# New durations in a planner's table, block sums of x on one engine, and a scaling step on either of two

## The chip, the cores and the metric

One NeuronCore of one Trainium2 chip runs the kernel. The metric is device time in microseconds (us) of one execution; lower is better. The engines are PE (TensorE), DVE (VectorE), ACT (ScalarE), POOL (GpSimd) and SP (the queue that issues most transfers). Each runs its own instructions strictly in the order in which the program wrote them.

## The reference

```python
def reference(q, k, v, n_sink, window, moe_*, moe2_*):
    x = attention(q, k, v)        # 2 batches, 8 heads, 768 rows, head size 64; window of 128 plus 4 sink columns
    x = x.reshape(1536, 512)
    # first mixture: every expert sees every row
    P = exp(x @ w_gate - max); P = 8 rounds of row and column scaling of P     # 1536 x 8
    x = sum(P[:, e:e+1] * (relu(x @ w1[e]) @ w2[e]) for e in range(8))         # 512 -> 1024 -> 512
    # second mixture: each row goes to one expert, 192 rows each, by a greedy pass over the sorted logits
    logits = x @ w_gate2
    out[rows of e] = relu(x[rows of e] @ w1b[e]) @ w2b[e]
```

All inputs and the output are float32.

## The kernel before

Rows of x are held in 12 tiles of 128 (the code's `t`), two tiles to a group of 256 columns, two groups to a pair `p` of 512. Every matmul operand is kept as a rounded high part and a low remainder (`hh`/`hl`, `w1hs`/`w1ls`, `xp[:, 0]`/`xp[:, 1]`), and each product is three matmuls: high by high, low by high, high by low. ACT makes high parts, DVE makes low parts by a subtraction.

The program runs through these stages. **Opening and attention**, over 12 tiles, with expert 0 of the first mixture woven in once two tiles of x are ready (`make_step`: first products G1 at L1037, second products G2 at L1068; `relu` and `hlo` make `hh` and `hl` at L1106 and L1109). Expert 0's output waits for the factors P: `cb` (L1082, ACT) copies it out of the accumulator, and `scale0` (L1089, DVE) multiplies it by P later. **Experts 1 to 5**, in 60 units (`make_unit`): the first product of a unit is seven block products of 2x2 blocks (L1272), which need sums and differences of blocks of x. `make_tx` makes these sums once for each of the three pairs p, eight 128x512 tensors for each (`to`: L1209 sums of a high and a low part, L1212 differences), and splits them into high and low (L1215 ACT, L1216 DVE). `split_blocks` does the same with the weights (L929 to L980). After a unit's products, ACT copies (`cp`, `cu`, L1288), DVE adds (`c`, L1296), ACT applies relu (L1329), DVE makes the low part (`hl`, L1332), and the second products follow (L1360). A unit's first product writes the buffer that the unit before has to have emptied, so PE waits there for the `hl<-hp` of L1332. **Experts 6 and 7**, in pairs (L1130), while DVE forms the second gate's logits (L1446, L1466). Then the **routing** rounds on DVE, with second products of expert 7 held back as cover for PE (L1068), rows scattered to memory by row number and read back, and the **second mixture**, 8 experts of 192 rows (L2025 to L2078). There an expert's two output halves are scattered by POOL (`out_dram`, L2102), with row numbers that DVE casts into `idx` (L1932); `idx` has three buffers, so the casts of an expert wait until the scatter of the expert three before has landed. Weights come in through SP, are split by ACT (L869) and DVE or POOL (L867) all along.

No order is written out by hand. Everything is a `task(engine, cost, function, deps, prio)`, and a planner (`Sched.run`), while the program is built, picks the next task by these costs; the order of the picks is the program order of each engine. A task may name two engines with two costs; the one on which it would end first gets it. The costs serve the planner alone: no instruction depends on them but through the order, the choice of engine, and this method, which puts transposes of the identity matrix (the fillers, L200) on PE where the planner expects PE to have nothing to do until time t:

```python
def warm(self, t):
    c = self.clock["PE"]
    free = [j for j in range(len(self.banks)) if self.banks[j] is not None and self.banks[j] <= c]
    per = 0.213 if c < COLD else 0.11
    n = int((t - c - 0.06) / per)
    if n < 1 or not (self.extra or free):
        return
    p = ps.tile([P, 512], F32, name=self.extra or self.names[free[0]])
    for _ in range(n):
        nc.tensor.transpose(p[:, :P], ident, ident)
```

A result reaches another engine `LAG` = 0.15 us after its cost has run (0.23 behind PE, 1.1 behind a transfer), in both kernels.

## Time and profile before

| what | us |
|---|---|
| median of 3 runs | 1386.44 |
| lowest and highest run | 1386.37, 1393.91 |
| the profiled execution, its own time | 1385.85 |
| its span, first to last instruction | 1383.9 |

All rows shown below come from the profiled execution; what lies around its span is 1385.85 - 1383.9 = 1.95 us. Its time is 0.6 us below the median. A row of the trace names the line of the code, the engine, the operation, output<-inputs, and partitions x elements; times in the timeline count from the start of the span.

### The profile page before, as it was taken

What the parts mean: (1) busy time and instruction counts of PE and PEld (TensorE: products, weight loads), DVE (VectorE), ACT (ScalarE), POOL (GpSimd) and SP (SyncE); (2) the same over time, 40 slices, a digit from 0 to 9 for tenths busy, and PEclk for the clock granted to TensorE, in tenths of its full rate; (3) what the DMA queues carried; (4) which work ended last, traced back from release to release, by engine and by line L of the source; (5) the groups of instructions that cost most, each with busy time, mean ns of one, the idle gap of its engine ahead of it and who ended that gap; (6) DMA issues with size and microseconds to landing.
All of it is one profiled execution on the core that took longest, in us unless ns stands there. A gap on an engine that the chain in (4) does not pass through costs nothing. (4 is left out here: it accounts for less than half of the span.)

```text
span 1383.9 us, 22562 instructions
## 1 busy us (share of the span) xinstructions
PE 1357.6 (98%) x8220; PEld 1166.5 (84%) x8220; DVE 940.0 (68%) x2538; ACT 622.8 (45%) x1570; POOL 124.2 (9%) x255
## 2 busy tenths in 40 slices
PE   8999999989999999999999999999999999999998
PEld 7888888879988888998888899888887777788876
DVE  8877765996364655546464645449999768578875
ACT  6877762544243433333342423331133353267764
POOL 3211110230000000000000000000001113410111
PEclk9999999999999999999999999999999999999999
DMA  7432311111020101011010101161020010478762
GB/s 177 123 83 57 85 39 39 62 49 59 16 62 1 62 16 47 16 46 47 16 49 14 62 1 61 46 200 41 16 92 16 1 46 17 118 248 273 244 218 70
DMA packets 102532, 101.50 MB, mean 73 GB/s; under 512 B 42248, under 2 KB 79112, under 8 KB 102288
## 3 DMA queue, kind: packets, MB, share of 16 engines
q1 hardware_dynamic: 100432, 93.71, 22.5%
q0 software_dynamic: 1984, 6.30, 1.4%
q8 instruction: 67, 1.10, 0.3%
q14 instruction: 49, 0.40, 0.1%
HBM read 91.71 MB, written 8.28 MB: 72 GB/s over the span
## 5 line engine op out<-in xcount | busy, mean ns | idle before, releaser
L1329 ACT ACTIVATE hh<-c 128x256 fp32r<-128x256 f32 x180 | 73.4, 414 | 128.0 <-DVE c L1296 114.9
L1130 PE MATMUL hp<-xp,w1hs 128*128 128x512 f32 x384 | 121.0, 396 | 0.0
L1296 DVE TENSOR_TENSOR c<-hp,cp 128x256 f32<-128x256 f32 x120 | 50.6, 422 | 101.2 <-PE hp L1272 100.3
L1360 PE MATMUL o<-w2ls,hh 128*128 128x512 f32 x240 | 95.1, 396 | 0.0
L1360 PE MATMUL o<-w2hs,hh 128*128 128x512 f32 x240 | 94.4, 393 | 0.0
L1360 PE MATMUL o<-w2hs,hl 128*128 128x512 f32 x240 | 94.3, 393 | 0.0
L1272 PE MATMUL hp<-xp,w1hs 128*128 128x256 f32 x480 | 89.1, 284 | 4.8 <-DVE hl L1332 4.5
L1272 PEld LDWEIGHTS hp<-xp,w1hs 128*128 128x128 f32 x480 | 78.1, 190 | 11.2 <-DVE hl L1332 5.6
L1535 POOL TENSOR_TENSOR hl<-h,hh 128x256 fp32r<-128x256 f32 x15 | 12.2, 815 | 803.4 <-ACT hh L1532 763.1
L1332 DVE SCALAR_TENSOR_TENSOR hl<-c,hh 128x256 fp32r<-128x256 f32 x180 | 76.6, 435 | 8.1 <-ACT hh L1329 5.3
L1130 PEld LDWEIGHTS hp<-xp,w1hs 128*128 128x128 f32 x384 | 69.4, 188 | 14.8
L1130 PE MATMUL hp<-xp,w1ls 128*128 128x512 f32 x192 | 75.9, 395 | 0.0
L1037 PE MATMUL hp<-xp,w1hs 128*128 128x256 f32 x384 | 74.0, 287 | 0.1
L1068 PE MATMUL o<-w2hs,hh 128*128 128x512 f32 x176 | 71.4, 406 | 0.0
L1068 PE MATMUL o<-w2hs,hl 128*128 128x512 f32 x176 | 69.9, 397 | 0.7 <-DVE hl L1109 0.6
L1068 PE MATMUL o<-w2ls,hh 128*128 128x512 f32 x176 | 70.0, 398 | 0.0
L1329 ACT ACTIVATE hh<-hp 128x256 fp32r<-128x256 f32 x60 | 23.1, 385 | 103.5 <-PE hp L1272 103.5
L867 DVE TENSOR_TENSOR w1ls<-w1r,w1hs 128x512 fp32r<-128x512 f32 x90 | 61.1, 688 | 11.8 <-ACT w1hs L869 11.1
L867 DVE TENSOR_TENSOR w2ls<-w2r,w2hs 128x512 fp32r<-128x512 f32 x89 | 59.2, 685 | 14.4 <-ACT w2hs L869 9.0
L1288 ACT ACTIVATE cu<-hp 128x256 f32<-128x256 f32 x60 | 22.9, 382 | 102.0 <-PE hp L1272 102.0
L1272 PE MATMUL hp<-xp,w1ls 128*128 128x256 f32 x240 | 68.1, 284 | 0.0
L1332 DVE SCALAR_TENSOR_TENSOR hl<-hp,hh 128x256 fp32r<-128x256 f32 x60 | 25.5, 424 | 59.9 <-ACT hh L1329 59.8
(490 smaller groups left out, 4067.0 us busy)
## 6 DMA issues: line engine op xcount, KB each, us to landing
w1r<-in_moe_w_dram SPq DMA_DIRECT2D x46, 512.0 KB, 4.3
w2r<-in_moe_w_dram SPq DMA_DIRECT2D x46, 512.0 KB, 4.4
wr<-in_moe_w_dram SPq DMA_DIRECT2D x46, 512.0 KB, 4.1
xs<-xs_d SPq DMA_DIRECT2D x14, 256.5 KB, 4.0
nk<-in_k_dram SPq DMA_DIRECT2D x12, 256.0 KB, 3.8
nq<-in_q_dram SPq DMA_DIRECT2D x12, 256.0 KB, 5.9
nv<-in_v_dram SPq DMA_DIRECT2D x12, 256.0 KB, 3.1
wgb<-wgd SPq DMA_DIRECT2D x1, 2048.0 KB
```

The source lines that it names most:

```text
L867: (nc.gpsimd if eng == "POOL" else nc.vector).tensor_tensor(lo[:, c], r[:, c], f32(hi[:, c]), op=OP.subtract)
L1037: nc.tensor.matmul(p, a, b, start=(c == 0 and j == 0), stop=(c == DC - 1 and j == 2), skip_group_check=True)
L1068: nc.tensor.matmul(OUTP[g, j], a_, b_, start=(first and i == 0), stop=(last and i == 2), skip_group_check=True)
L1130: nc.tensor.matmul(HS[k, 0].rearrange("p a b -> p (a b)"), a, b, start=(c == 0 and j == 0), stop=(c == DC - 1 and j == 2), skip_group_chec ...
L1272: nc.tensor.matmul(st[bk], l_[:, c], r_[:, c], start=(start and c == 0 and j == 0), stop=(c == 1 and j == 2), skip_group_check=True)
L1288: act(st[key], st[bk], AF.Copy)
L1296: tt(st[out], st[bk], st[key], op=OP.add)
L1329: act(hh, st[key], AF.Relu)
L1332: nc.vector.scalar_tensor_tensor(HT[i, f, t][1], st[key], 0.0, f32(HT[i, f, t][0]), op0=OP.max, op1=OP.subtract)
L1360: nc.tensor.matmul(OUTP[g, j % GT], a_, b_, start=(first and f == 0 and z == 0), stop=(last and f == 1 and z == 2), skip_group_check=True)
L1535: (nc.gpsimd if eng == "POOL" else nc.vector).tensor_tensor(HT[s][1], h32_of(g, fc), f32(HT[s][0]), op=OP.subtract)
```

## The change

Almost all costs in the planner's table are replaced. On DVE and ACT they rise: a 128x512 subtraction from 0.61 to 0.69, one of 128x256 from 0.34 to 0.43, ACT's 128x512 copies from 0.48 to 0.60 or from 0.52 to 0.63, the 128x256 ones from 0.27 or 0.31 to 0.39, the attention's small steps likewise. On PE those of the first expert, of the pairs and of the second mixture rise by some 6 to 9% (G2: 0.2157 to 0.2325 a matmul); the costs of the units' products (0.703 and 1.395), of POOL's subtractions (`PSP` 1.35) and of transfers stay. Two tasks change in kind: the block sums of x may no longer go to POOL, and the scaling of expert 0's output may go to ACT.

```diff
-        l0 = task("DVE", 0.61, lambda: low(0), deps=a + d, prio=pr, use=[KH[t]], name="klo")
+        l0 = task("DVE", 0.69, lambda: low(0), deps=a + d, prio=pr, use=[KH[t]], name="klo")
...
-            nms = [task(("DVE", "ACT"), (0.20, 0.30) if n == 1 else (0.27, 0.42), lambda eng, hp=hp, hh=hh: nm(eng, hp, hh), deps=[r], prio=pr, use=[eh, sth], name="norm")
+            nms = [task(("DVE", "ACT"), (0.28, 0.40) if n == 1 else (0.355, 0.51), lambda eng, hp=hp, hh=hh: nm(eng, hp, hh), deps=[r], prio=pr, use=[eh, sth], name="norm")
...
-                    l = task(("DVE", "POOL"), (0.61, PSP), lambda eng, k=k, c=c: sp(k, c, True, eng), deps=[a],
+                    l = task(("DVE", "POOL"), (0.69, PSP), lambda eng, k=k, c=c: sp(k, c, True, eng), deps=[a],
...
-                def scale0(j=j, t=t):
+                def scale0(eng, j=j, t=t):
                     a0 = acc[g][:, j, :DM]
-                    ts(a0, a0, PR[:, t, 0:1], None, op0=OP.mult)
+                    if eng == "ACT":
+                        act(a0, a0, AF.Copy, scale=PR[:, t, 0:1])
+                    else:
+                        ts(a0, a0, PR[:, t, 0:1], None, op0=OP.mult)
...
-                    CB[t] = task("DVE", 0.4, scale0, deps=[z, SKH[0]], prio=v_gem(NG * NU * 2 + s % 48), name="sc0")
+                    CB[t] = task(("DVE", "ACT"), (0.45, 0.62), scale0, deps=[z, SKH[0]], prio=v_gem(NG * NU * 2 + s % 48), name="sc0")
...
-            def go(eng):
+            def go():
...
-                f(nc.gpsimd if eng == "POOL" else nc.vector, s3(sm[nm]))
+                f(nc.vector, s3(sm[nm]))
 
-            x = task(("DVE", "POOL"), (0.61, PSP), go, deps=[SW["task"]] + [z[0] for z in deps], prio=pr + 0.1 * k,
+            x = task("DVE", 0.69, go, deps=[SW["task"]] + [z[0] for z in deps], prio=pr + 0.1 * k,
```

What follows for the order: fillers rise from 146 to 249. Of the 24 block sums, POOL had 11 and now has none. Of the 12 scalings DVE had all and now has 3. POOL takes 8 weight subtractions (L867) more from DVE, ACT 8 of DVE's normalizations of attention (L622), and DVE 11 copies of the transposed attention weights (L647) from ACT.

Vector engine, in units 1 and 2, from the add that ends a block product of unit 1 to the `hl<-hp` that unit 2's first product waits for; `sA`, `sB`, `wr`, `t` are block sums of x, `tx` and `xp` their low parts, `c` and `hl` belong to the unit. Before (the sums at L1209 and L1212 that don't stand here were POOL's):

```order
L1296 TENSOR_TENSOR c_3819<-hp_3735,cp_3798 128x256
L1212 TENSOR_TENSOR sB<-sA,wr 128x512
L1296 TENSOR_TENSOR c_3833<-side_3778,cu_3785 128x256
L1332 SCALAR_TENSOR_TENSOR hl<-c_3819,hh 128x256
L1216 TENSOR_TENSOR tx_3208<-wr,tx_3208 128x512
L1216 TENSOR_TENSOR tx_3208<-sB,tx_3208 128x512
L1216 TENSOR_TENSOR xp_122<-t_3837,xp_122 128x2x256
L1332 SCALAR_TENSOR_TENSOR hl<-hp_3735,hh 128x256
```

The same place in the changed kernel, vector engine again (lines from L1090 on stand three further down in it):

```order
L1299 TENSOR_TENSOR c_3895<-hp_3793,cp_3875 128x256
L1215 TENSOR_TENSOR wr<-wr,sA 128x512
L1299 TENSOR_TENSOR c_3908<-side_3858,cu_3865 128x256
L1335 SCALAR_TENSOR_TENSOR hl<-c_3895,hh 128x256
L1212 TENSOR_TENSOR sA<-xp_122 128x512
L1219 TENSOR_TENSOR tx_3219<-wr,tx_3219 128x512
L1335 SCALAR_TENSOR_TENSOR hl<-hp_3793,hh 128x256
```

Between the first add and the `hl<-hp` there were three low parts and one difference; there are one low part, one sum and one difference now, and the other sums stand ahead of or behind the piece.

TensorE, at the step from unit 1's first two block products to its third (`hp0<-tx0,ehs`); `av` is the second product of the unit before. Before:

```order
L1360 MATMUL av_3759<-w2hs2_143,hh_3711 128x512
L1360 MATMUL av_3759<-w2ls2_144,hh_3711 128x512
L1360 MATMUL av_3759<-w2hs2_143,hl_3712 128x512
L1360 MATMUL av_3759<-w2hs2_143,hh_3700 128x512
L1360 MATMUL av_3759<-w2ls2_144,hh_3700 128x512
L1360 MATMUL av_3759<-w2hs2_143,hl_3701 128x512
L1272 MATMUL hp0_3735<-tx0_3207,ehs1_3203 128x256 x2
```

The same step on TensorE in the changed kernel:

```order
L1363 MATMUL av_3815<-w2hs2_143,hh_3764 128x512
L1363 MATMUL av_3815<-w2ls2_144,hh_3764 128x512
L1363 MATMUL av_3815<-w2hs2_143,hl_3765 128x512
L1363 MATMUL av_3815<-w2hs2_143,hh_3748 128x512
L1363 MATMUL av_3815<-w2ls2_144,hh_3748 128x512
L1363 MATMUL av_3815<-w2hs2_143,hl_3749 128x512
L200 MATMUL side0_3834<-ident_82 128x128 x16
L1275 MATMUL hp0_3793<-tx0_3218,ehs1_3214 128x256 x2
```

Sixteen fillers stand ahead of the third block product where there were none. In all, units 0 to 3 had 17 fillers and have 62; the later units had none and have eight times 2; ahead of the first G1 there were 114 and are 152.

Vector engine, second mixture, from the output of the fifth expert (`yb`) to the casts of the row numbers of the eighth (`idx`), which wait for that output's scatter. Before:

```order
L2098 TENSOR_TENSOR yb<-side_15901,yb 64x512
L867 TENSOR_TENSOR w2ls_136<-w2r,w2hs_135 128x512
L867 TENSOR_TENSOR w1ls_138<-w1r,w1hs_137 128x512
L867 TENSOR_TENSOR w2ls_136<-w2r,w2hs_135 128x512
L867 TENSOR_TENSOR w2ls_140<-w2r,w2hs_139 128x512
L2042 TENSOR_TENSOR sm<-av,t_16170 128x192
L867 TENSOR_TENSOR w2ls_140<-w2r,w2hs_139 128x512
L2051 SCALAR_TENSOR_TENSOR hs<-sm,hs 128x128
L2052 SCALAR_TENSOR_TENSOR hs<-sm,hs 128x64
L2042 TENSOR_TENSOR sm<-side_16161,t_16181 128x192
L1932 CAST idx_16207<-xs_15772 128x1
L1932 CAST idx_16209<-xs_15774 64x1
```

Vector engine in the changed kernel, the twelve rows that end with the same casts (the fifth expert's `yb` stands nine rows ahead of the first of them):

```order
L867 TENSOR_TENSOR w1ls_138<-w1r,w1hs_137 128x512
L2054 SCALAR_TENSOR_TENSOR hs<-sm,hs 128x128
L2055 SCALAR_TENSOR_TENSOR hs<-sm,hs 128x64
L867 TENSOR_TENSOR w1ls_138<-w1r,w1hs_137 128x512
L2045 TENSOR_TENSOR sm<-side_16282,t_16334 128x192
L867 TENSOR_TENSOR w2ls_140<-w2r,w2hs_139 128x512
L2054 SCALAR_TENSOR_TENSOR hs<-sm,hs 128x128
L2055 SCALAR_TENSOR_TENSOR hs<-sm,hs 128x64
L867 TENSOR_TENSOR w2ls_140<-w2r,w2hs_139 128x512
L2045 TENSOR_TENSOR sm<-hp_16321,t_16359 128x192
L1935 CAST idx_16374<-xs_15902 128x1
L1935 CAST idx_16376<-xs_15904 64x1
```

The second cast moved from 11 to 20 rows behind the `yb` whose scatter it waits for; between them stand seven subtractions of `hs` and `sm` steps more and one weight subtraction more.

## Rows read from the trace of the kernel before

**Rows 1.** The page: busy time, share of the span and instructions of each engine

```profile
PE 1357.6 (98%) x8220; PEld 1166.5 (84%) x8220; DVE 940.0 (68%) x2538; ACT 622.8 (45%) x1570; POOL 124.2 (9%) x255
```

**Rows 2.** Stages by the windows view; its columns stand in its first line

```profile
core 0: us, PE busy (x) PEld busy (x) DVE busy (x) ACT busy (x) POOL busy (x), PEclk, DMA share, GB/s
0.00:40.00 40.00, 33.93 (x260) 28.82 (x261) 36.04 (x126) 28.98 (x72) 12.64 (x30) 1.00 0.73 166
40.00:245.00 205.00, 203.44 (x1548) 174.87 (x1548) 147.11 (x533) 139.01 (x360) 27.61 (x118) 1.00 0.25 69
245.00:302.00 57.00, 51.51 (x312) 44.66 (x311) 56.05 (x106) 26.74 (x62) 19.07 (x13) 0.94 0.14 47
302.00:1042.00 740.00, 740.00 (x4361) 652.36 (x4360) 443.49 (x1019) 244.72 (x610) 0.53 (x1) 1.00 0.15 48
...
1190.00:1225.00 35.00, 31.73 (x153) 26.05 (x152) 16.70 (x39) 11.84 (x27) 11.09 (x21) 0.95 0.72 202
...
1320.00:1340.00 20.00, 17.43 (x93) 14.97 (x92) 14.59 (x38) 12.23 (x30) 3.02 (x3) 0.91 0.55 180
```

**Rows 3.** The fillers' line in 0 to 40 us, windows view of L200

```profile
0.00:40.00 40.00, 17.13 (x114) 14.43 (x114) 1.00 0.73 166
```

**Rows 4.** One burst of fillers in the timeline of PE

```profile
269.52 1.58 PE L200 MATMUL side<-ident 128*128 128x128 f32 x13
```

**Rows 5.** Whom PE waited for: us in total, times, longest

```profile
PE hp L1272 <- DVE hl L1332: 4.5, 2, 3.0
PE hp L2070 <- DVE hs L2051: 2.6, 1, 2.6
...
PE side L1068 <- PEq L1783: 1.9, 1, 1.9
PE av L2025 <- DVE xe L1975: 1.4, 1, 1.4
```

**Rows 6.** Timeline of PE behind its longest wait

```profile
284.99 0.80 PE L1272 MATMUL hp<-xp,w1hs 128*128 128x256 f32 x2 [3.01 <-DVE hl L1332]
...
288.14 0.63 PE L1360 MATMUL av<-w2ls,hh 128*128 128x512 f32 x1
288.57 0.63 PE L1360 MATMUL av<-w2hs,hl 128*128 128x512 f32 x1
```

**Rows 7.** Timeline of DVE ahead of that wait's end

```profile
279.27 1.73 DVE L1212 TENSOR_TENSOR sB<-sA,wr 128x512 f32<-128x512 f32 x1
...
282.72 0.68 DVE L1216 TENSOR_TENSOR tx<-wr,tx 128x512 fp32r<-128x512 f32 x1
283.32 0.68 DVE L1216 TENSOR_TENSOR tx<-sB,tx 128x512 fp32r<-128x512 f32 x1
```

**Rows 8.** Timeline of POOL at the same time

```profile
279.16 1.29 POOL L1212 TENSOR_TENSOR t<-sA,wr 128x512 f32<-128x512 f32 x1 [5.10 <-DVE sA L1209]
```

**Rows 9.** DVE's groups by line and shape, 245 to 302 us

```profile
L1332 DVE SCALAR_TENSOR_TENSOR hl<-c,hh 128x256 fp32r<-128x256 f32 x9 | 6.6, 745 | 0.1
L1212 DVE TENSOR_TENSOR sB<-sA,wr 128x512 f32<-128x512 f32 x3 | 5.3, 1762 | 0.0
...
L1089 DVE TENSOR_SCALAR acc<-acc,PR 128x512 f32<-128x512 f32 x8 | 3.5, 479 | 0.0
...
L1332 DVE SCALAR_TENSOR_TENSOR hl<-hp,hh 128x256 fp32r<-128x256 f32 x3 | 1.2, 415 | 0.1
```

**Rows 10.** Timeline of DVE, fourth expert's scatter and the casts behind it

```profile
1298.58 0.67 DVE L2098 TENSOR_TENSOR yb<-hp,yb 64x512 f32<-64x512 f32 x1
...
1303.35 0.15 DVE L1932 CAST idx<-xs 64x1 int32<-64x1 f32 x1 [0.17 <-DMA out_dram<-yb,idx]
```

**Rows 11.** Timeline of DVE, fifth expert's scatter and the casts behind it

```profile
1319.60 0.68 DVE L2098 TENSOR_TENSOR yb<-side,yb 64x512 f32<-64x512 f32 x1 [0.17 <-ACT yb L2095]
...
1327.09 0.15 DVE L1932 CAST idx<-xs 64x1 int32<-64x1 f32 x1 [2.88 <-DMA out_dram<-yb,idx]
```

**Rows 12.** Timeline of PE at the same time

```profile
1328.22 0.62 PE L2070 MATMUL hp<-w2hs,hs 128*128 128x512 f32 x1 [2.57 <-DVE hs L2051]
```

More of the change, by code (lines that the diff above doesn't have):

```diff
@@ L605, in neg @@
                 ts(ST[t][:, 1, s2], ST[t][:, 0, s2], -scale, None, op0=OP.mult)
-            ng = task("DVE", 0.07, neg, deps=ms, prio=pr, use=[sth], name="neg")
-            exs = [task("ACT", 0.41 if n == 1 else 0.51, f, deps=[ng], prio=pr, use=[eh, sth], name="exp") for f in xs]
+            ng = task("DVE", 0.21, neg, deps=ms, prio=pr, use=[sth], name="neg")
+            exs = [task("ACT", 0.58 if n == 1 else 0.70, f, deps=[ng], prio=pr, use=[eh, sth], name="exp") for f in xs]
             def rc(s2=s2):
@@ L995, in split_blocks @@
[L995 to L996 removed]
+        a01 = task("ACT", 0.63, h01, deps=dd, prio=pr, use=u, name=f"hi{n}")
+        a2 = task("ACT", 0.39, h2, deps=dd + [a01], prio=pr + 0.1, use=u, name=f"hi{n}")
+        b01 = task("DVE", 0.69, l01, deps=[a01], prio=pr, use=u, name=f"lo{n}")
+        c1 = task("DVE", 0.43, s1, deps=dd + [a01], prio=pr + 0.1, use=u + [sA], name=f"s{n}")
@@ new lines, in split_blocks @@
+        c3 = task("DVE", 0.43, s3, deps=dd + [a01], prio=pr + 0.2, use=u + [sB], name=f"s{n}")
+        c2 = task("DVE", 0.43, s2, deps=[c1, c3], prio=pr + 0.3, use=u + [sA, sB], name=f"s{n}")
+        c4 = task("DVE", 0.43, s4, deps=[c2], prio=pr + 0.4, use=u + [sA, sB], name=f"s{n}")
+        ae = task("ACT", 0.63, he, deps=[c2, c3], prio=pr + 0.4, use=u + [sB], name=f"hi{n}")
+        a3 = task("ACT", 0.39, h3, deps=[c1], prio=pr + 0.45, use=u + [sA], name=f"hi{n}")
+        a6 = task("ACT", 0.39, h6, deps=[c4], prio=pr + 0.46, use=u + [sA], name=f"hi{n}")
@@ L1109, in low @@
             nc.vector.scalar_tensor_tensor(HT[s][1], HS[s], 0.0, f32(HT[s][0]), op0=OP.max, op1=OP.subtract)
-        a = task("ACT", 0.27, relu, deps=[prev], prio=pr - 33.0, use=[hph, hh_], name="relu")
-        b = task("DVE", 0.34, low, deps=[a], prio=pr - 33.0, use=[hph, hh_], name="hlo")
+        a = task("ACT", 0.39, relu, deps=[prev], prio=pr - 33.0, use=[hph, hh_], name="relu")
+        b = task("DVE", 0.43, low, deps=[a], prio=pr - 33.0, use=[hph, hh_], name="hlo")
         make_g2(s, hh_, [a, b], pr + 7, steps[s])
@@ L1153, in low @@
                 nc.vector.scalar_tensor_tensor(HT[s][1], HS[k, 0][:, i], 0.0, f32(HT[s][0]), op0=OP.max, op1=OP.subtract)
-            a = task("ACT", 0.27, relu, deps=[prev], prio=pr - 33.0 + i, use=[hph, hh_], name="relu")
-            b = task("DVE", 0.34, low, deps=[a], prio=pr - 33.0 + i, use=[hph, hh_], name="hlo")
+            a = task("ACT", 0.39, relu, deps=[prev], prio=pr - 33.0 + i, use=[hph, hh_], name="relu")
+            b = task("DVE", 0.43, low, deps=[a], prio=pr - 33.0 + i, use=[hph, hh_], name="hlo")
             make_g2(s, hh_, [a, b], pr + 8 + i, (e, 2 * p + i, n, f, first, last), GT * i)
@@ L1332, in low @@
                 nc.vector.scalar_tensor_tensor(HT[i, f, t][1], st[key], 0.0, f32(HT[i, f, t][0]), op0=OP.max, op1=OP.subtract)
-            x = task("ACT", 0.31, relu, deps=[src], prio=pr - 33.0, use=[rr, hh_], name="relu")
-            y = task("DVE", 0.34, low, deps=[x], prio=pr - 33.0, use=[rr, hh_], name="hlo")
+            x = task("ACT", 0.39, relu, deps=[src], prio=pr - 33.0, use=[rr, hh_], name="relu")
+            y = task("DVE", 0.43, low, deps=[x], prio=pr - 33.0, use=[rr, hh_], name="hlo")
             B_ALL.extend([x, y])
@@ L1388, in make_restore @@
         x = task("SP", 1.5, back, deps=dep, prio=pr, use=[h], name="b12")
-        y = [task("ACT", 0.57, lambda z=z: act(b12_of(p)[:, z], sm["r"][:, z], AF.Copy), deps=[x], prio=pr, use=[h], name="b12") for z in range(2)]
+        y = [task("ACT", 0.63, lambda z=z: act(b12_of(p)[:, z], sm["r"][:, z], AF.Copy), deps=[x], prio=pr, use=[h], name="b12") for z in range(2)]
         B12[p] = y
@@ L1535, in lo @@
             (nc.gpsimd if eng == "POOL" else nc.vector).tensor_tensor(HT[s][1], h32_of(g, fc), f32(HT[s][0]), op=OP.subtract)
-        a = task("ACT", 0.30, hi, deps=[H32[g, fc]], prio=pr, use=[hh_], name="hhi")
-        return a, task(("DVE", "POOL"), (0.34, PLO), lo, deps=[a], prio=pr, use=[hh_], name="hlo")
+        a = task("ACT", 0.41, hi, deps=[H32[g, fc]], prio=pr, use=[hh_], name="hhi")
+        return a, task(("DVE", "POOL"), (0.43, PLO), lo, deps=[a], prio=pr, use=[hh_], name="hlo")
     DEF = []
```

124 lines of the change are left out of this document (57 added, 67 removed).

## The prediction

> **What bounds the kernel now.** I read the page's engine shares first: TensorE is busy for 1357.6 us of a span of 1383.9, 98% [rows 1], so the most that any better order can give back is its idle time, 26.3 us, and what it works at a lowered clock. The windows by stage say where that lies [rows 2]; the reader is to take "us" less "PE busy" in each. The opening, 0 to 40 us, has 6.1 us of it, attention 1.6, the step from attention to the units, 245 to 302 us, 5.5, the units from 302 to 1042 us none at all, the routing's start 3.3, and one stretch of the second mixture 2.6. The granted clock is below one in three of them: 0.94 of 57 us, so (1 - 0.94) x 57 = 3.4 us more at the most (the last digit is rounded; I take 3.0), 0.95 of 35 us, 1.7, and 0.91 of 20 us, 1.8. The timeline shows the first of these: two neighbouring products stand 0.43 us apart behind the long wait [rows 6], against a planner's cost of 0.2325 for one such matmul.
>
> Then I read the list of waits, for who is late in each of these stretches [rows 5]. In the step to the units it is DVE's `hl` of L1332, two waits of 4.5 us together, the longest 3.0; in the second mixture DVE's `hs`, 2.6 us once; at the routing a branch on TensorE's queue, 1.9 us, and DVE's `xe`, 1.4. So DVE matters at four places, and in 740 us of the units it doesn't: it is busy there for 443 us beside a TensorE that never waits. In the step to the units DVE is the bound: 56.05 us busy of 57, with ACT at 26.7 and POOL at 19.1 [rows 2].
>
> **Opening.** Fillers ahead of the first G1 go from 114 to 152. The old ones took 17.13 us [rows 3], 0.150 each, so 38 more want 38 x 0.150 = 5.7 us. TensorE idles for 6.1 us there while DVE is busy for 36.0 of 40, and DVE's work up to the second tile's `xl` is the same before and after. So they can lie wholly in idle time (0), or, since the planner now thinks DVE slower than it may be, all stand ahead of products that are ready (+5.7). I take a quarter, **+1.5**.
>
> **Attention and expert 0.** Eight normalizations go from DVE to ACT, eleven evictions from ACT to DVE, eight weight subtractions to POOL. TensorE idles for 1.6 of 205 us, with DVE at 147 and ACT at 139 [rows 2], so the cover for these is there: **0**. If the other order opens gaps it costs some 3 us, about twice the idle time that is there now; nothing can give back more than 1.6.
>
> **Step to the units.** POOL's eleven block sums now run on DVE. What one costs there: two low parts of the same shape stand 0.60 us apart, though each is shown as 0.68 long [rows 7], so 11 x 0.60 = 6.6 us are added. What goes: of twelve scalings nine leave for ACT; eight of them took 479 ns as shown [rows 9], the shown length running over the next one as above, so I take 0.40 each: -3.6. ACT has 30 us free and takes them at a cost of nothing. And DVE's own operations were long while POOL ran: a difference took 1.73 us [rows 7] in the moment in which POOL's ran for 1.29 [rows 8], against 0.68 alone. Over the stretch three differences have a mean of 1762 ns and nine low parts `hl<-c` of 745, where the undisturbed `hl<-hp` has 415 [rows 9]: 3 x (1.762 - 0.68) + 9 x (0.745 - 0.415) = 6.2 us of stretching. If each of the eleven sums stretched something by the same 1.1 us, it is 11 x 1.1 = 12.1. So DVE has 6.6 - 3.6 - 6.2 = 3.2 us less, at most 9.1 less; the weight subtractions that go to POOL lie elsewhere mostly. On the piece that the order shows, between the add of unit 1 and `hl<-hp`, one sum, one low part and one difference stand where three low parts and a stretched difference stood, some 2 us less against a wait of 3.0. With the whole stretch relieved by 3 us or more I expect the 5.5 us of idle and the 3.0 of lowered clock, 8.5 in all, to go but for 0.5.
>
> The Trainium skill, "Perfetto Trace Analysis" ("Optimizing Scalar/DVE Operations"), holds that moving work between DVE and GpSimd might not help, since the two share a port, and "Trainium Architecture — The Big Picture" ("What this means for kernel authors") calls that an exclusive lock. The rows above agree, 1.73 us of DVE beside 1.29 of POOL, and by that rule taken strictly the eleven sums would free 11 x 1.29 = 14.2 us of DVE instead of 6.2.
>
> What takes their place: 17 fillers in units 0 to 3 become 62. A burst of 13 takes 1.58 us [rows 4], 0.12 each, so 45 x 0.12 = 5.4 us, and these are on TensorE's path whenever DVE is in time. Where they now stand, TensorE's own wait was 3.0 us in one place, so some would have been idle anyway; I count them in full against the stall taken as gone: -8.0 + 5.4 = **-2.6** (from -8.5, fillers in what is left of the idle time, to +5.4, nothing gained).
>
> **Units and pairs.** Eight times two fillers stand in units that had none, where TensorE never waits: 16 x 0.12 = 1.9. Four more ahead of the pairs, 0.5. Together **+2.4**. No cover hides them: DVE has 300 us free there.
>
> **Routing.** Between its rounds 12 second products of expert 7 stand where 13 did, and the cover behind the last is 75 matmuls instead of 69, 6 x 0.2325 = 1.4 us more. The branch's wait of 1.9 us has nothing to do with these; the 1.4 us on `xe` [rows 5] can be covered by them. I take **-1**, from -3.3 (all idle time of that stretch) to +3.3 (as much again).
>
> **Second mixture.** Row numbers for the eighth expert's scatter wait until the fifth's has landed. The wait on DVE is 2.88 us, to 1327.09, 7.5 us behind the start of the `yb` at 1319.60 [rows 11]; with the fourth the landing let the cast go 4.8 us behind its `yb`, almost without waiting [rows 10]. Behind the waiting cast stands the `hs` that TensorE wants, hence 2.57 us of idle [rows 12] and 1.8 of lowered clock, 4.4 together. Ten rows between the `yb` and the cast took 7.5 - 2.9 = 4.6 us, 0.46 each; with nine more the cast comes 4.6 + 9 x 0.46 = 8.7 us behind the `yb`, later than either landing. So the wait goes, and what was idle becomes work: **-4.0** (from -4.4 to +3.0, if another queue head takes that place with the same wait and the clock stays). The margin is 8.7 - 7.5 = 1.2 us.
>
> **Sum.** 1.5 + 0 - 2.6 + 2.4 - 1 - 4.0 = -3.7 against the profiled execution's 1385.85 gives 1382.1; the median of the runs is 0.6 above it, so **1382.8** as a median. A measurement of this kernel tells about 1% from no change, 13.9 us; this forecast is within it.
>
> **Rivals.** (A) *The fillers are paid in full.* The planner now holds a DVE step of 128x512 for 0.69 us where two stand 0.60 apart [rows 7], so it thinks results 15% later than they are and puts fillers ahead of products that are ready. Then the opening pays 5.7, units 0 to 3 pay 5.4, the rest 2.4, and if the step's stall shrinks by no more than its lowered clock (-3.0) while routing and second mixture give 5.0, the sum is 13.5 - 3.0 - 5.0 = +5.5: 1391.4, as a median **1392**. The point from which it decides: with the fillers at 13.5 and 5.0 given back elsewhere, the kernel is slower wherever the step gives back less than 8.5, all that there is in it; with the opening's fillers hidden, less than 2.8. For it: fillers are the one thing that the change surely adds to the busiest engine. Against it: TensorE idles at both places now. [...]
>
> (B) *All stalls go and the fillers fall into idle time.* Step -8.5, second mixture -4.4, routing -3.3, units +2.4: -13.8, 1372.1, as a median **1372.6**. For it: DVE is the bound of the step and gets up to 9 us. Against it: in units 0 to 3 the places with fillers would have to be where TensorE waits still, and with DVE relieved it doesn't.
>
> (C) *Stalls move.* The order of the second mixture differs in every row, and another cast meets its scatter: -4.0 becomes 0, the rest stays at +0.3: 1386.2, as a median **1386.8**, no change. For it: a margin of 1.2 us, and landings that differ by 2.7 us between two experts. Against it: of all casts only one waited long.
>
> (D) *The table does nothing but reorder*, the block sums gaining what their DVE time costs; the step then keeps its 8.5 us and pays 5.4 of fillers beside it: 1382.1 + 8.0 = 1390.1, median **1391**. It shares its time with A and I count them together.
>
> **How the numbers follow.** Forecast 0.45 (1378 to 1386), C 0.18, A and D 0.23, B 0.14. The range is to hold eight in ten. Below, B at its end and half a point of fillers hidden in the opening give 1371; above, A with the attention's 3 us gives 1395. The chance of faster by over 1% (under 1372.6) is half of B and a little of the forecast's lower tail, 0.10; slower by over 1% (over 1400) needs A and a second mixture that loses its 3 us too, 0.06; within 1%, 0.84.
>
> **What would show it.** In the profile after: for the step, PE idle under 1 us between 245 and 302 us with DVE's differences at 0.7 us instead of 1.76, and the wait on `hl<-hp` gone from the list; fillers at 62 in that place. For the second mixture, no wait on `out_dram` at the eighth expert's cast and a clock of 1.00. For the opening, the start of the first G1 no more than 2 us later. The forecast is wrong if the first G1 starts 5 us later, if the wait on `hl` is as long as before beside the fillers, or if a new wait of over 3 us stands in attention, where I looked for none.

## The result, and the profile after

The changed kernel takes 1376.97 us (median of 4 runs, 1375.76 to 1378.61). Runs of the kernel before, taken beside it, have a median of 1389.92 (1386.37 to 1393.91). The ratio is 0.9912, with a 95% interval of 0.9889 to 0.9935: 0.9% faster, 13 us. Beside the later experiments, 15 to 17 runs of the kernel before at a time have medians of 1386.83 to 1388.90; against these it would be 10 to 12 us. The two profiled executions are 7.2 us apart, 1385.85 and 1378.61; the profile of before is below all four of the runs of before, that of after is the highest of its four. The longer runs of one kernel tend to have the lower granted clock: those of e3 below took 1373.07 us at a mean of 0.998 and 1378.45 at 0.995, while all four of the changed kernel had 0.998. All stage figures below come from profiled executions.

The page's first section, engine shares over the span of 1376.8 us:

```profile
PE 1357.8 (99%) x8323; PEld 1172.4 (85%) x8323; DVE 936.8 (68%) x2536; ACT 628.5 (46%) x1576; POOL 112.8 (8%) x251
```

TensorE's busy time is what it was [rows 1], 1357.8 against 1357.6, although it holds some hundred fillers more; the idle time has gone from 26.3 to 19.0 us. The windows by stage, in the columns of [rows 2]:

```profile
0.00:40.00 40.00, 34.42 (x284) 30.52 (x285) 35.75 (x119) 27.21 (x69) 13.06 (x30) 1.00 0.67 154
40.00:245.00 205.00, 203.64 (x1552) 174.54 (x1551) 148.71 (x524) 139.92 (x360) 33.46 (x124) 1.00 0.26 72
245.00:302.00 57.00, 56.03 (x384) 51.27 (x384) 50.84 (x113) 31.73 (x69) 4.20 (x3) 1.00 0.15 47
302.00:1042.00 740.00, 740.00 (x4365) 651.94 (x4364) 443.82 (x1012) 247.23 (x613) 1.40 (x2) 1.00 0.15 48
1190.00:1225.00 35.00, 32.07 (x161) 27.04 (x160) 18.15 (x40) 13.88 (x31) 8.16 (x16) 0.95 0.66 194
1320.00:1340.00 20.00, 20.00 (x117) 17.59 (x116) 17.43 (x48) 15.52 (x38) 2.24 (x4) 1.00 0.72 231
```

In the step to the units the idle time fell from 5.5 to 1.0 us, the clock rose to 1.00 and POOL has almost nothing left; in the second mixture the idle time is gone. In the list of waits, where [rows 5] had `hl` with 4.5 us and `hs` with 2.6, DVE's `hl` and `hs` stand no more (one wait of 1.1 us is for ACT's `hs`); the longest are now

```profile
PE o L1068 <- PEq L1786: 2.9, 1, 2.9
PE o L200 <- DVE ident L277: 2.1, 1, 2.1
PE side L2072 <- ACT hs L2050: 1.1, 1, 1.1
```

DVE's groups between 245 and 302 us, which answer to [rows 9]:

```profile
L1335 DVE SCALAR_TENSOR_TENSOR hl<-c,hh 128x256 fp32r<-128x256 f32 x9 | 3.8, 417 | 0.2 <-ACT hh L1332 0.2
...
L1215 DVE TENSOR_TENSOR sB<-sA,wr 128x512 f32<-128x512 f32 x3 | 2.0, 683 | 0.0
```

The stretching is gone: 417 ns where the mean was 745, 683 where it was 1762. But that stretch of TensorE is not free of fillers; its timeline holds several bursts, the longest three

```profile
270.86 1.80 PE L200 MATMUL side<-ident 128*128 128x128 f32 x15
...
275.27 1.91 PE L200 MATMUL side<-ident 128*128 128x128 f32 x16
...
288.26 2.02 PE L200 MATMUL side<-ident 128*128 128x128 f32 x17
```

To see where the time went I compare the start of the same instruction in each trace: the first G1 (L1037), the first block product (L1272), the `hl<-hp` of the sixth unit, the first L1501 of the second gate, the first L2025 of the second mixture, and the end. What each stretch between two of these is longer (+) or shorter (-) than in the profile of before, in us:

| kernel (its median / ratio to runs of before beside it) | opening | attention, expert 0 | step | units, pairs | gate, routing | second mixture | span |
|---|---|---|---|---|---|---|---|
| after (1376.97 / 0.991) | +1.8 | -0.5 | -4.0 | +1.6 | -2.6 | -3.4 | -7.1 |
| e1 both kinds, old costs (1377.59 / 0.993) | 0.0 | -1.0 | -6.9 | 0.0 | -1.4 | +1.5 | -7.9 |
| e2 new costs alone (1383.30 / 0.997) | +1.8 | -0.1 | -2.6 | +1.6 | -2.1 | -4.2 | -5.6 |
| e3 after, no fillers behind the opening (1376.67 / 0.992) | +1.8 | -1.4 | -4.4 | -0.1 | +0.7 | -5.0 | -8.3 |
| e4 before, 4 idx buffers (1382.41 / 0.996) | +1.0 | +0.4 | +1.0 | 0.0 | -1.3 | -3.1 | -2.0 |
| e5 before's plan, sums on DVE (1385.10 / 0.999) | +0.3 | -0.8 | -2.7 | 0.0 | +0.5 | +2.6 | -0.1 |
| e6 sums on DVE, replanned (1377.50 / 0.993) | +0.9 | -1.1 | -7.1 | 0.0 | -1.1 | +1.0 | -7.3 |
| e7 both kinds, 4 idx buffers (1374.62 / 0.992) | +1.0 | -1.1 | -6.9 | 0.0 | +0.1 | -4.1 | -11.1 |
| e8 both kinds, TensorE's new costs (1402.75 / 1.011) | -0.2 | +4.6 | -9.2 | +4.5 | +5.3 | +12.7 | +17.9 |
| e9 scaling alone (1384.38 / 0.997) | +0.4 | -0.1 | -3.2 | 0.0 | +1.4 | +2.6 | +1.1 |
| e10 e8 and 4 idx buffers (1386.43 / 0.998) | +0.1 | +3.8 | -9.1 | +3.1 | +8.4 | -3.8 | +2.5 |
| e11 both kinds, DVE's and ACT's new costs (1407.88 / 1.014) | +7.6 | +2.5 | +2.6 | +2.3 | +0.9 | +2.2 | +18.1 |
| e12 both kinds, new costs late, 4 idx buffers (1374.97 / 0.990) | 0.0 | -1.1 | -6.8 | 0.0 | -1.8 | -1.2 | -10.9 |

How far one profile of each can be trusted shows in e4, whose order is that of before on every engine: up to the sixth unit its three stretches differ by +1.0, +0.4 and +1.0 with no cause in the kernel. Differences under 1.5 us in one stretch are read as nothing, unless several kernels repeat them.

### The profile page after: what moved, and what is told of

It is laid out like the page before. It is cut to its first block, busy times and chain, and to the rows that moved or that the text cites. A ratio compares the mean times of both kernels' runs of the same rounds, so it can differ in the third digit from the quotient of the medians.

```text
span 1376.8 us, 22702 instructions
## 1 busy us (share of the span) xinstructions
PE 1357.8 (99%) x8323; PEld 1172.4 (85%) x8323; DVE 936.8 (68%) x2536; ACT 628.5 (46%) x1576; POOL 112.8 (8%) x251
## 5 line engine op out<-in xcount | busy, mean ns | idle before, releaser
L1363 PE MATMUL o<-w2ls,hh 128*128 128x512 f32 x240 | 95.1, 396 | 0.0
L1363 PE MATMUL o<-w2hs,hh 128*128 128x512 f32 x240 | 94.4, 393 | 0.0
L1363 PE MATMUL o<-w2hs,hl 128*128 128x512 f32 x240 | 94.3, 393 | 0.0
L1037 PE MATMUL hp<-xp,w1hs 128*128 128x256 f32 x384 | 75.2, 289 | 0.1
L1068 PE MATMUL o<-w2hs,hh 128*128 128x512 f32 x168 | 68.4, 407 | 2.9 <-PEq L1786 2.9
L1068 PE MATMUL o<-w2ls,hh 128*128 128x512 f32 x168 | 66.9, 398 | 0.0
L1068 PE MATMUL o<-w2hs,hl 128*128 128x512 f32 x168 | 66.6, 396 | 0.0
L867 DVE TENSOR_TENSOR w1ls<-w1r,w1hs 128x512 fp32r<-128x512 f32 x86 | 59.0, 692 | 10.7 <-ACT w1hs L869 10.0
L869 ACT ACTIVATE w1hs<-w1r 128x512 fp32r<-128x512 f32 x92 | 57.1, 624 | 12.1 <-DMA w1r<-in_moe_w_dram 12.0
```

The source lines that it names most:

```text
L867: (nc.gpsimd if eng == "POOL" else nc.vector).tensor_tensor(lo[:, c], r[:, c], f32(hi[:, c]), op=OP.subtract)
L869: act(hi[:, c], r[:, c], AF.Copy)
L1037: nc.tensor.matmul(p, a, b, start=(c == 0 and j == 0), stop=(c == DC - 1 and j == 2), skip_group_check=True)
L1068: nc.tensor.matmul(OUTP[g, j], a_, b_, start=(first and i == 0), stop=(last and i == 2), skip_group_check=True)
L1363: nc.tensor.matmul(OUTP[g, j % GT], a_, b_, start=(first and f == 0 and z == 0), stop=(last and f == 1 and z == 2), skip_group_check=True)
```

## The experiments

**e1 and e2: the two halves of the change.** The kinds alone (sums on the vector engine, scaling on either; for it costs of 0.40 and 0.48) and the new table alone. In e1:

```diff
-            x = task(("DVE", "POOL"), (0.61, PSP), go, ...
+            x = task("DVE", 0.61, go, ...
-                    CB[t] = task("DVE", 0.4, scale0, ...
+                    CB[t] = task(("DVE", "ACT"), (0.40, 0.48), scale0, ...
```

and in e2 all other lines of the change, with `(0.69, PSP)` for the sums and 0.45 for the scaling on the vector engine.

> All costs as before; only the two changes of kind: the block sums all on the vector engine, the scaling on either engine. The order differs from that of before in the step from attention to the units alone (the first 1055 rows and the last 7372 of TensorE are the same), with 28 fillers there instead of 17. Theory (relief of the vector engine makes the gain in the step): idle time of TensorE between 245 and 302 us from 5.5 to under 2.5 us, granted clock 1.00 there, the kernel 3 to 5 us faster than before, and the second mixture keeps its wait of 2.6 us on hs. Rival (the new costs, which space things out, make the gain in the step too): 0 to 1 us faster, idle time of 4 us or more in the step.

> The new costs alone: block sums may go to POOL (it gets 14), the scaling stays on the vector engine. The order equals that of the changed kernel in the first 993 rows of TensorE and the last 7435, so only the step from attention to the units differs. Theory: the opening, the routing and the second mixture as in the changed kernel (no wait on hs at the eighth expert, 4 us given back from 1043 us on to the end and 2 us more ahead of the routing, 2 us lost in the opening), but the step keeps 4 us or more of idle time or lowered clock: the kernel 2 to 4 us faster than before, 3 to 5 us slower than the changed kernel. Rival (the costs alone do everything, the kinds nothing): as fast as the changed kernel within 1 us, idle time in the step under 1.5 us.

The windows of e1, and of e2 behind it, for the step:

```profile
245.00:302.00 57.00, 56.82 (x374) 51.18 (x374) 54.07 (x117) 34.79 (x77) 2.92 (x3) 1.00 0.18 59
```

```profile
245.00:302.00 57.00, 50.38 (x327) 44.38 (x326) 55.12 (x104) 27.03 (x61) 21.83 (x16) 1.00 0.14 47
```

0.2 us of idle time against 6.6: the kinds make the gain in the step, more of it (-6.9 and -1.0 ahead of it) than expected and more than the whole change has there (-4.0 and -0.5); the span is 7.9 us shorter where I had expected 3 to 5. The table alone brings the second mixture (-4.2) and the routing, as expected, and charges +1.8 in the opening and +1.6 in the units. Ratios of 0.9927 (0.9908 to 0.9946) and 0.9967 (0.9951 to 0.9983) agree with that order, though e1 kept the wait on `hs`, 3.5 us in its list.

**e3: are the fillers paid for?** The planner's own clock is left as it is, only the transposes are not issued:

```diff
-            for _ in range(n):
+            for _ in range(n if c < 48.0 else 0):
                 nc.tensor.transpose(p[:, :P], ident, ident)
```

> The changed kernel without its 97 fillers behind the opening (1 in attention, 62 in units 0 to 3, 16 in later units, 16 around the routing, 2 in the second mixture); order of all else the same. Theory (in units 0 to 3 the fillers lie in time in which TensorE would wait anyway; in later units they are paid for): 16 x 0.11 = 1.8 us back in the units, up to 2 us back in the step to the units, idle time of 5 us between 245 and 302 us where there was 1: 2 to 4 us faster than the changed kernel, if the clock stays at 1.00; if idle time lowers the clock there, no faster. Rival (the fillers are paid in full): 97 x 0.11 = 10.7 us faster than the changed kernel.

Where after had fillers in the step, e3 waits; its list of waits from 245 to 302 us:

```profile
PE hp L1275 <- DVE hl L1335: 2.3, 2, 1.2
PE side L1275 <- DVE xp L1219: 1.2, 1, 1.2
PE side L775 <- DVE cs L765: 1.0, 1, 1.0
PE hp L1275 <- ACT ehs L969: 0.5, 1, 0.5
PE hp L1275 <- DVE els L973: 0.4, 1, 0.4
```

It is 51.58 us busy there, idle for 5.4; after spent 7.8 us on fillers and idled for 1.0. In the stretch of the step, from which the 62 fillers went, e3 is 0.4 us shorter than after (-4.4 against -4.0); up to the sixth unit it is 1.3 us ahead, the rest of that in attention, where one filler went. Both are within the scatter, against the 62 x 0.12 = 7.4 that the fillers would cost at the price of [rows 4]. In the units it gets 1.6 us back, as expected: nothing covers those. At the routing it loses 3.3 us against after. The windows show where, 1205 to 1215 us, e3 first, after behind it:

```profile
1205.00:1215.00 10.00, 9.77 (x32) 8.11 (x31) 2.54 (x5) 1.83 (x4) 2.34 (x4) 0.55 0.48 160
```

```profile
1205.00:1215.00 10.00, 10.00 (x57) 8.54 (x55) 4.58 (x8) 3.29 (x6) 2.28 (x4) 1.00 0.58 186
```

Both kernels have a pause of TensorE of 2.9 us shortly before, and behind it a granted clock of 0.50, the lower of its two levels, or little more. In after the pause ends at 1199.80, on a branch, with products behind it, and after 1203.5 the clock is back at full. In e3, some 4 us earlier in its work here, it ends at 1204.56, on a read of rows, with transposes behind it, and the clock stays at 0.50 to 1213.5; the same eight transposes take 2.72 us instead of 1.52. The windows behind the pause and the timeline of TensorE in e3:

```profile
1205.00:1213.50 8.50, 8.50 (x27) 7.13 (x27) 2.25 (x4) 1.15 (x2) 2.34 (x4) 0.50 0.41 133
```

```profile
1204.56 2.72 PE L1987 MATMUL side<-ident,xs 128*128 128x128 f32 x8 [2.85 <-DMA xs<-xs_d]
```

and in after:

```profile
1199.80:1203.50 3.70, 3.70 (x9) 2.88 (x10) 2.44 (x6) 1.46 (x3) 0.33 (x2) 0.54 0.31 39
```

```profile
1199.80 0.49 PE L1068 MATMUL o<-w2hs,hh 128*128 128x512 f32 x1 [2.93 <-PEq L1786]
...
1208.44 1.52 PE L1987 MATMUL side<-ident,xs 128*128 128x128 f32 x8
```

The sixteen fillers around the routing stood elsewhere in after, eight at 1122 us and eight at 1214. So the loss is one of a pause and a low clock; that the missing fillers made it is not shown. The medians, 1376.67 against 1376.97, show no gain; in the profile the expected 2 to 4 us are spent again at the routing. The rival, 10.7 us, is out.

**e4: the second mixture's wait.** A fourth buffer in the kernel before, nothing else:

```diff
-                i = rkp["p"].tile([m, 1], I32, name=f"idx{n}", bufs=3)
+                i = rkp["p"].tile([m, 1], I32, name=f"idx{n}", bufs=4)
```

> The kernel before with a fourth buffer for the row numbers idx; its order is that of before. Theory (the cast of the eighth expert waits for the fifth's scatter, and hs and TensorE behind it): no wait on out_dram at the cast, none of 2.6 us on hs, granted clock 1.00 between 1320 and 1340 us, 3.5 to 4.4 us faster than before. Rival (another wait on the vector engine takes its place there): less than 1.5 us faster, with a wait of over 1 us on hs left in that stretch.

DVE's timeline, the fifth expert's `yb` and the eighth's casts:

```profile
1321.40 0.68 DVE L2098 TENSOR_TENSOR yb<-side,yb 64x512 f32<-64x512 f32 x1 [0.17 <-ACT yb L2095]
...
1325.88 0.31 DVE L1932 CAST idx<-xs 128x1 int32<-128x1 f32 x2
```

The casts go through 4.5 us behind the `yb` without a wait, the longest wait on `hs` is 0.4 us, the clock from 1320 to 1340 is 1.00, and the second mixture is 3.1 us shorter. Ratio 0.9962 (0.9948 to 0.9976). This stretch is a little under the expected 3.5, the medians beside each other (1387.78 and 1382.41) are 5.4 us apart, above the expected 4.4; the rival is out.

**e5 and e6: POOL's sums, without and with a new plan.** In e5 the planner still chooses as before, and the function ignores its choice; in e6 it knows.

```diff
-                f(nc.gpsimd if eng == "POOL" else nc.vector, s3(sm[nm]))
+                f(nc.vector, s3(sm[nm]))
```

> The kernel before with its own plan, so with every engine's order as before, but the eleven block sums that the plan gives to POOL run on the vector engine, at the place in its queue that the plan's order gives them. The scaling stays on the vector engine. Theory (a POOL block sum stretches what the vector engine does meanwhile by about 1.1 us, so POOL's help costs as much as it saves): the stretched operations go (differences at 0.68 us instead of 1.76), the vector engine is as busy as before between 245 and 302 us within 2 us, the step's idle time moves by less than 2 us either way. Rival (no contention counts; the sums are plain extra work on the engine that bounds the step): vector engine 6.6 us more in the step, the step 4 us or more slower.

> All costs as before and the scaling on the vector engine; only the block sums are all on it, with a new plan. The order differs from before in the step to the units alone. Theory (relief by both parts; the sums' part is 6.6 us more work against 6 to 12 us of stretching gone, the scaling's part 3.6 us less work): the sums alone give back 1 to 4 us of the step's 7.9, the rest needs the scaling on the scalar engine; idle time in the step of 2 to 4 us. Rival (the sums are all of it): within 1.5 us of the kernel with both kinds. Other rival (the scaling is all of it): no faster than before within 1 us.

Windows of the step, e5 and then e6:

```profile
245.00:302.00 57.00, 52.45 (x336) 45.97 (x335) 56.16 (x125) 28.42 (x65) 3.17 (x3) 1.00 0.16 52
```

```profile
245.00:302.00 57.00, 57.00 (x381) 51.94 (x380) 56.30 (x126) 29.47 (x67) 3.56 (x3) 1.00 0.15 47
```

The vector engine's 56.16 us in e5 against 56.05 before say little, since it is nearly full in both windows and does 19 instructions more in that of e5. The whole run tells more; e5's page:

```profile
PE 1358.6 (98%) x8220; PEld 1168.2 (84%) x8220; DVE 937.1 (68%) x2549; ACT 622.5 (45%) x1570; POOL 106.8 (8%) x244
```

With the eleven sums on top and all else the same, it is busy for 937.1 us against 940.0 [rows 1]; e4, with the order of before, has 939.5. Up to the sixth unit's `hl<-hp` it is 254.4 against 257.3, the same 2.9 us. So the stretching that went is more than what the sums add, and the `sB<-sA,wr` that had a mean of 1762 ns has

```profile
L1212 DVE TENSOR_TENSOR sB<-sA,wr 128x512 f32<-128x512 f32 x3 | 2.1, 692 | 0.0
```

TensorE's idle time in the window is 4.6 us, with 4.0 of it still on `hl`: 0.9 less than before, within the expected 2. So the theory holds, with more stretching than it had; the step is 2.7 us shorter, with a clock of 1.00 where before had 0.94. The runs show no difference (0.9968 to 1.0006). In e6, where nothing but the planner's knowledge is added, TensorE idles for 0.0 us (with 29 fillers there, 3.8 us, where e5 has 16). Up to the sixth unit's `hl<-hp` the vector engine does the same 812 instructions in e5 and e6, in 254.4 and 253.8 us of busy time, and comes to that `hl` at 328.1 us in e5, at 324.0 in e6: only their order differs. I had expected 1 to 4 us from it and got 7.1 and 1.1 ahead of it: the whole of what both kinds give. My theory fell here, and the first rival holds.

**e7: do the gains add?** e1 with the edit of e4.

> Both changes of kind with the costs of before, and a fourth buffer for the row numbers: 7.9 us in the step (as the kernel with both kinds) and 3 to 5 us in the second mixture (as the fourth buffer alone). Theory (the two stalls are independent): 10.5 to 13 us faster than before, 3 to 4 us faster than the changed kernel. Rival (they share a cause, or one comes back elsewhere): no faster than the changed kernel.

They do: -6.9 in the step, -4.1 in the second mixture, a span of 1372.8 against 1376.8 after. The median, 1374.62 (1373.88 to 1378.3), is 2.4 us below that of the changed kernel, taken beside other runs; the ratio of 0.9921 (0.9893 to 0.9949) cannot tell the two apart.

**e8, e10 and e11: one half of the table at a time.** e8 is e1 with the twelve lines of TensorE's costs new, vector and scalar engine old; e11 is the opposite; e10 is e8 with the edit of e4. One line of each half:

```diff
 e8:
-                y = task("PE", 0.2157 * len(parts), ...
+                y = task("PE", 0.2325 * len(parts), ...
 e11:
-            l = task(("DVE", "POOL"), (0.61, PSP), ...
+            l = task(("DVE", "POOL"), (0.69, PSP), ...
```

> Both changes of kind; of the costs only those of TensorE are the new ones, vector and scalar engine keep the old ones (0.61 for 128x512, the distance of two operations in the trace). Fillers: 106 ahead of the first G1, 9 in the units, 11 later. Theory (it is the lengthened costs of vector and scalar engine that cost 1.8 us in the opening, 1.6 us in the units and 2.9 us in the step, since they lengthen what the planner waits for beyond what the trace shows): the opening as before or earlier within 0.7 us, no loss in units, the step gives 6 us or more; and the second mixture keeps a wait, since that order came with the costs of the vector engine. 8 to 11 us faster than before. Rival (TensorE's own new costs do the harm): opening 1.5 us later, step under 5 us.

> The kernel with both kinds and TensorE's new costs alone, which was 18 us slower than the kernel with both kinds, and a fourth buffer for the row numbers. There the casts of experts 3 to 7 stand 3, 11, 8, 8, 8 rows behind the output whose scatter they wait for (before 19, 33, 18, 13, 11; changed kernel 41, 35, 32, 29, 20), and the vector engine waited 13.7 us at them. Theory (in the second mixture these waits are the loss): the second mixture gets back 10 us or more of the 12.7 us that it lost against before, and what is left of the loss lies ahead of 1227 us. Rival (TensorE there waits for hs itself, because vector and scalar engine are planned too close behind it): less than 6 us back.

> Both kinds; of the costs only those of vector and scalar engine are the new ones, TensorE keeps the old ones, the opposite of the last. Fillers: 376 instead of 249 (174 ahead of the first G1, 17 in attention, 88 in units 0 to 3, 16 in later units, 13 around the routing, 68 in the second mixture). Theory (what counts is how the engines' costs stand to each other: with vector and scalar engine held too slow beside TensorE, casts and low parts come late enough that TensorE waits for nothing, but fillers stand in front of matmuls that are ready): hardly a wait in the second mixture, its 68 fillers and the 17 of attention paid in full, 85 x 0.11 = 9.4 us, and 1 to 3 us more in the step: 8 to 14 us slower than the changed kernel. Rival (fillers lie in time in which TensorE would wait): within 3 us of the changed kernel.

e8 was expected 8 to 11 us faster than before, since 0.61 is near the 0.60 that lie between two operations of the vector engine [rows 7]. It is 1.1% slower (1.0079 to 1.0145). The opening and the step do as expected (-0.2 and -9.2); attention, pairs, routing and second mixture lose 27 us together. In the last of these DVE's list of waits, from 1215 us on, shows what:

```profile
DVE idx L1935 <- DMA out_dram<-yb,idx: 8.4, 5, 2.1
...
DVE idx L1935 <- DMA out_dram<-ya,idx: 5.3, 4, 3.6
```

and e10 takes these away: its second mixture is 16.5 us shorter than e8's and equal to that of the other kernels with four buffers. The casts that e8 put 3 to 11 rows behind the outputs were the loss there. The losses ahead of it stay.

e11 is slower by 1.4% (1.0116 to 1.0153) and 31 us over the changed kernel; I had expected 8 to 14. TensorE waits for `hs` no more, as expected, and with 68 fillers, 68 x 0.11 = 7.5 us, the second mixture is at +2.2 where after is at -3.4. The step is 6.6 us longer than after's (+2.6 against -4.0) where I had expected 1 to 3. What I had not expected at all is the opening: +7.6 us. The vector engine's `xl` of the second tile, which the first G1 needs, starts at

```profile
44.40 0.69 DVE L693 TENSOR_TENSOR xp<-av,xp 128x512 fp32r<-128x512 f32 x1
```

in e11, and at 38.17 in e8, 40.13 after and 38.32 before. In e11 133 instructions of the vector engine stand ahead of it, 40.4 us of busy time; in e8 and before 119, 34.2 and 34.4 us.

**e9: the scaling alone.** The kernel before with

```diff
-                    CB[t] = task("DVE", 0.4, scale0, ...
+                    CB[t] = task(("DVE", "ACT"), (0.40, 0.48), scale0, ...
```

> All costs as before, block sums on either of vector engine and POOL (10 go to POOL); only the scaling may go to the scalar engine. The order differs from before in the step to the units alone. Theory, after the sums alone gave back all 8 us of the step: the scaling has no part in it, POOL's help has; so this kernel keeps the stretched operations and waits, and the step (with what lies ahead of it) changes by less than 1.5 us. Rival (each part alone relieves the vector engine enough): the step gives back 4 us or more.

-3.2 us in the step: less than the rival's 4, more than the theory's 1.5. TensorE idles for 57 - 52.87 = 4.1 us, `hl` has 2.5 us of waits instead of 4.5, and `sB<-sA,wr` is still stretched, to a mean of 1055 ns. So the scaling does relieve the engine; it only adds nothing where the sums have left POOL already (e1 and e6 are alike). The runs are 0.3% faster (0.9955 to 0.9990), though the profiled span is 1.1 us longer.

**e12: costs of before up to the pairs, new ones behind, and four buffers.** e7, with the change's own costs in every line from the second gate's on, for example

```diff
-            b = task("DVE", 0.47, lo, ..., name="xelo")
+            b = task("DVE", 0.56, lo, ..., name="xelo")
```

> Both kinds; the costs of before for all tasks up to the last unit and the pairs (no loss in opening and units, 7.9 us back in the step), the new costs for the second gate, the routing and the second mixture, and a fourth buffer for the row numbers. Theory (the gains of the parts add): as the kernel with both kinds and the fourth buffer, 12 us faster than before, and 1 to 3 us more from the second gate on: 1371 to 1374 us. Rival (the end of the program wants the order that both halves of the table together give): 1375 us or more.

1374.97 (1374.79 to 1376.24), ratio 0.9900 (0.9881 to 0.9918): the best ratio of all, but a microsecond over the theory's range and at the rival's edge. Its span of 1373.0 is that of e7. The new costs give nothing at the end that the fourth buffer hasn't given: with four buffers the second mixture is -4.1 under the old costs and -1.2 under these.

## Why the prediction was right, and where its steps were not

The forecast was 1382.8, within the noise of no change; measured were 1376.97, inside the range and on the side that the forecast leaned to. Every sign that it named for the step, the second mixture and the opening stands in the profile of after. Yet the sum came out near for reasons that are partly luck: the second mixture went by the mechanism that was named, the opening's and the step's terms were near without it. Of the difference, 5.8 us, 3.5 are the sum's (the profiles are 7.2 us apart where the sum had 3.7); 0.6 I added for the median of before, and the profile of after lies 1.6 above its median. The ratio speaks of 13 us since the runs of before beside it were slower than its profile, up to 1393.91. Some of that is the second mixture: four other kernels with the order of before in it (e1, e5, e6, e9) took 1.0 to 2.6 us longer there than the profile of before. Where the remainder of this scatter, and the granted clock that goes with it, comes from stays open.

Term by term:

**Opening, +1.5: measured +1.8, by another path.** I let a quarter of the added fillers be paid ahead of a vector engine with unchanged work. What is seen is that the vector engine's `xl` comes 1.8 us later (38.32 to 40.13), and with it the first G1. The sentence that failed is "DVE's work up to the second tile's `xl` is the same": it is 119 instructions in both, but busy for 34.4 us before and 35.8 after. One copy of attention weights more and one normalization less stand there, and two of the copies are twice as wide as those of before:

```profile
31.54 0.69 DVE L647 COPY eT<-hp 128x512 f32<-128x512 f32 x1 [0.77 <-PE hp L642]
...
33.70 0.69 DVE L647 COPY eT<-side 128x512 f32<-128x512 f32 x1 [0.26 <-PE side L642]
```

They cannot be all of it, since the first tile's `xl`, ahead of both, is 1.4 us late already (before, then after):

```profile
26.37 0.68 DVE L693 TENSOR_TENSOR xp<-av,xp 128x512 fp32r<-128x512 f32 x1
```

```profile
27.79 0.69 DVE L693 TENSOR_TENSOR xp<-av,xp 128x512 fp32r<-128x512 f32 x1 [0.49 <-ACT xp L692]
```

That it comes with the new costs of vector and scalar engine, and not with TensorE's, is shown by e11 and e8. Whether the opening's own fillers have a part in it was not tested: e3 keeps them, and the two copies wait for transposes of TensorE that stand behind fillers. That the term came out near is luck.

**Attention and expert 0, 0: measured -0.5**, within the scatter.

**Step, -2.6: measured -4.0, two errors against each other.** Without fillers (e3) the step gives back 4.4 us where I had 8.0, and the fillers cost 0.4 where I had 5.4; that these nearly cancel is luck. The direction on the vector engine was right, the size of the stretching too small: with 0.60 us for each of eleven sums, as I had it, and 2.9 us less in all (e5), it was 6.6 + 2.9 = 9.5 us where I had 6.2, at most 12.1. By the Trainium skill's exclusive lock taken strictly ("Trainium Architecture — The Big Picture", "What this means for kernel authors") it would have been 14.2, and 14.2 - 6.6 = 7.6 us less; the trace agrees with the sign and not with this size. What failed is, first, "With the whole stretch relieved by 3 us or more I expect the 5.5 us of idle and the 3.0 of lowered clock, 8.5 in all, to go but for 0.5": e5 has that relief and keeps 4.6 us of idle time, while e6, with the same instructions on the vector engine in another order, idles for nothing. So a vector engine busy for 56.05 of 57 us had work that could wait and work that could not, and beside its load the place of the `hl` in its queue counted. A likely reason, not shown by itself, is that the planner put down 1.35 us of POOL for each of its sums and nothing for what it costs the vector engine, 9.5 / 11 = 0.9 us, so `hl` came later than it thought. Second, "I count them in full": e3 shows that of the 7.4 us at most 1.3 are paid. The waits were not gone in the changed kernel, as I had written, but covered: when the fillers are taken away, 1.0 us of idle time becomes 5.4. So what rival B says of the fillers holds for the step; rival A falls with that, rival D with the gain of the step, and rival C with the second mixture.

**Units and pairs, +2.4: measured +1.6.** The sixteen fillers are paid in full, as e3 shows; the price of 0.12 was a little high, and the four others lie behind the start of the second gate (L1501), in the next stretch.

**Routing, -1: measured -2.6.** From the first L1501 to the last it is 1.5 us shorter, a term that I did not have: the second gate's waits on `hl` (L1535), 0.9 us together before, stood below the list that I used and are gone.

```profile
PE side L1503 <- DVE hl L1535: 0.5, 2, 0.3
PE o L1503 <- DVE hl L1535: 0.4, 1, 0.4
```

The branch's wait grew from 1.9 to 2.9 us, and the last piece, from the first transposes of rows (L1984) to the first L2025, is 2.0 us shorter, without the wait on `xe`; but e1 and e4, which keep the order of before there, have -1.7 and -1.3 in it, so little of that can be put down to the change. The windows from 1060 to 1100 us, before and after:

```profile
1060.00:1100.00 40.00, 39.03 (x189) 28.17 (x188) 36.52 (x111) 16.06 (x52) 6.84 (x8) 1.00 0.01 1
```

```profile
1060.00:1100.00 40.00, 40.00 (x199) 30.16 (x198) 35.33 (x105) 16.43 (x52) 3.88 (x5) 1.00 0.01 1
```

**Second mixture, -4.0: measured -3.4** (-4.0 from the first L2069 on), by the mechanism that was named. I put the last casts 8.7 us behind the fifth `yb`; they are 8.6 behind, without a wait:

```profile
1316.78 0.68 DVE L2101 TENSOR_TENSOR yb<-o,yb 64x512 f32<-64x512 f32 x1 [0.42 <-ACT yb L2098]
...
1325.36 0.33 DVE L1935 CAST idx<-xs 128x1 int32<-128x1 f32 x2
```

e4 shows nearly the same gain with the order of before and one buffer more, so the table's part in it is to have pushed the casts back.

**What the new durations are worth.** The kinds alone make the gain of the whole change (1377.59 against 1376.97); the table pays 3.4 us in opening and units and 2.9 in the step for 6 or so in routing and second mixture. Rival A's basis, that 0.69 is too long beside a distance of 0.60, was the thought behind e8, and e8 turned it down: with true distances on two engines and new costs on TensorE alone the kernel lost 18 us, and the other half alone lost 18 too. Why balanced tables do better, too short on all engines or too long on all, was argued from these three runs and one table of waits, not shown by itself. What is shown is that either half alone moves casts and low parts: the casts too close behind the outputs in e8 (e10), the low part too late in the opening in e11.

## What to carry to other kernels

In a kernel that a planner orders, its costs count by how they stand to each other; change them for all engines or for none, and look afterwards for the few instructions at the head of a queue (a cast that waits for a transfer, a low part that the next product needs), which one more buffer may cure more cheaply than any table. That an engine is busy 98% of a stretch does not say that its load is the bound; look which of its instructions the waiting engine wants, and what stands ahead of it that could wait. Count fillers by place: where the engine would wait they cost here no more than the scatter can hide, where it would not they cost all of it.

## What the runs showed of the hardware beyond what was expected

Work that moved from GpSimd to the vector engine cost it less than nothing: with 11 operations of 128x512 more and the order otherwise the same, its busy time over the run went from 940.0 to 937.1 us (e5), since neighbours of 1762 ns went back to 692. A pause of TensorE costs more than itself, and not always the same: behind one of 2.93 us the changed kernel's clock was low for 3.7 us (0.54), behind one of 2.85 us that of e3 was at 0.50 for 8.9 us, though TensorE was busy without a gap in both; what makes the difference is open.
